# Stage 3 of a fused attention and gating kernel: leftover columns, product outputs and gate steps issued in another order

## The chip, the cores and the metric

The kernel runs on one core of a Trainium2 chip. The metric is the device time of one execution in microseconds; the kernel before took 685.45 us (median of 3 runs, 685.35 to 686.27). Every matmul is in 32-bit floats or in pairs of rounded high and low parts, so that a product of two such pairs is three matmuls.

## The reference

Three layers run one after the other on 4 batches of 576 rows. The change lies in the third.

```python
def reference(**kwargs):                      # cut
    attn_out = _attn_ref(q, k, v)             # rotary attention, 8 heads of 64
    x = _moe_ref(x=x, ...)                    # gated MLP with mixing over the rows
    return _moe2_ref(x=x, ...)

def _moe2_ref(x, w_gate, wq, wk, wv, wo):     # 4 experts, head width 64
    logits = x @ w_gate                       # the two best experts of each row, softmax over them: w
    for e in range(E):
        q, k, v = x @ wq[e], x @ wk[e], x @ wv[e]
        scores = scale * (q @ k.T), causal    # 576 x 576
        a = softmax(scores)
        ye = a @ v @ wo[e]
        out += (mask of e) * w * ye
```

## The kernel before

Stage 3 works through 8 units, n = 0 to 7: unit n is batch n // 2 and one pair of its four experts. A unit has 9 slots, x = 0 to 8, one for each block of 128 query rows of an expert (rows 512 to 575 of both experts share block 8). `slot3` writes out slot k = 9n + x. In it, in this order: `exps` of block x (ScalarE), the parked second halves of side products (`after`: evictions from PSUM, which also start the DMAs that fill q and k of the next unit), `scores` of block x + 1 and `turn` of block x - 1 (TensorE; the turn transposes the exponentials through a PSUM tile ps_t, of which there are two), `masked` of block x + 1 (VectorE: mask and maximum), `high` and `low` of block x - 1 (ScalarE copies the turned block to h1h or h0xh, VectorE writes the rounding error to h1l or h0xl). Then come the steps with the previous unit p, side products of other units (projections to q and k into the single two-bank tile ps_S, to values into ps_f and others, the output product into ps_f, ps_o or ps_S) and a few steps of the gates.

What the change touches:

- `gather` (VectorE) copies block 8's 64 leftover columns beside themselves, `turn_left` (TensorE) transposes them into a ps_t tile, `left_parts` makes the tile ht from them (ScalarE copy, VectorE subtraction). In the previous unit's block 8 this happens in slots 0 and 1.
- `av(True, 0)` and `av(True, 1)` are the second-half products with the values for the two experts of unit p, in slots 1 and 3; ps_o is a single PSUM tile. `av_out` empties it: ScalarE copies half of it to tmp, VectorE adds tmp to the other half, into xt. The last matmul of an `av` reads ht.
- `factor` makes the row factors rs (ScalarE, VectorE, four small GpSimd products with the gates wgt); `turn_factor` transposes them into ps_o's spare columns; `spread_factor` copies them to rr (ScalarE), stores rr in DRAM (d<-rr) and loads it back spread over the partitions (three DMAs r<-d).
- `finish(0)` and `finish(1)` (GpSimd) multiply xt by r and write the parts zh and zl, in slots 4 and 5 (unit 1: in 7 and 8). The output product `Output.blocks` reads them; in units 2, 4 and 6 its first two blocks, of the batch just ended, are side products of slots 6 and 7.
- `vproj` ends in seven steps for the gates: a subtraction (GpSimd), two comparisons (VectorE), two reductions and a subtraction into wgt (VectorE, GpSimd), an exponential of wgt (ScalarE), two more on VectorE, a sum and reciprocal, a product (GpSimd). Units 2, 4 and 6 run one step a slot.

ScalarE, VectorE, GpSimd and TensorE keep the order in which the program issues their instructions (the `Engine` wrapper pins it). DMAs issued on SP are not pinned in stage 3: a planner places each in SP's queue when it takes the DMA's inputs to be ready, the earlier in the program first. The queue itself runs in order, and a DMA that waits holds those behind it.

Unit 2 differs from units 3 to 7 in where its q and k projections stand: `QK_AT` spreads them over slots 0, 1, 3, 3, 4, 4, where the others have them in slots 0, 0, 2, 2, 3, 3. So in unit 2 half of a projection (6 matmuls) stands in slot 1, none in slot 2, and q is evicted (hi by ScalarE, lo by VectorE, then six DMAs q<-hi, qz<-hi, q<-lo) in slot 2, where the others do it in slot 1.

Of the kernel before, what the change touches and what calls it, by code (L numbers as in the profile page):

```python
# [15 lines left out]
B, H, S, D = 4, 8, 576, 64  # L16
# [27 lines left out]
def fused_kernel(ctx, tc, qk, v, w_in, w_out, w_sg, g_ln, b_sg, wqk, wvg, wo, rope, cst, out):  # L44
# [27 lines left out]
    def bank(t):  # L72
        shape = [P, 2, 512] if t.isupper() else [P, 512]
        return ps[t].tile(shape, F32, tag="b", name="ps_" + t)
# [195 lines left out]
    def parts_of(b):  # L270

        ts = []

        def load(c):
            t = xtile[0]()
            nc.sync.dma_start(t[:, 0:S], yd[b][c])
            nc.sync.dma_start(t[:, S:640], yd[b][c][:, 512:S])
            ts.append(t)

        for c in range(2):  # L280
            load(c)
            yield
        yp[b] = [ypools[b % 2].tile([P, 4, 640], F32R, tag="y" + x, name="y" + x) for x in "hl"]
        for c in range(4):
            split(yp[b][0][:, c], yp[b][1][:, c], ts[c])
            if c < 2:
                load(c + 2)
            yield
# [57 lines left out]
    with ExitStack() as st:  # L346
# [279 lines left out]
        works = {0: Work(), 1: Work()}  # L626
# [28 lines left out]
        for k in range(9 * B * NP + 7):  # L655
            n, x = divmod(k, 9)
# [27 lines left out]
    def qkproj(n, x):  # L684

        b, pp = divmod(n, 2)
        yh, yl = yp[b]
        hi = one.tile([P, S], F32R, tag="hi", name=f"hi{x}")
        lo = (ld if x else one).tile([P, S], F32R, tag=f"lo{x}", name=f"lo{x}")
        sl = slice((2 * x + pp) * P, (2 * x + pp) * P + P)  # L690
        t = bank("S")
        for x_ in mm3(halves(t), [(wq[0][:, c, sl], wq[1][:, c, sl], yh[:, c], yl[:, c]) for c in range(4)]):
            if n:
                yield
        if n == 0:
            yield
        pv = t[:, :, 0:HS]
        if x == 0:
            ACT.activation(hv(hi), pv, AF.Copy, scale=0.125)
            DVE.scalar_tensor_tensor(hv(lo), pv, 0.125, f(hv(hi)), op0=ALU.mult, op1=ALU.subtract)  # L700
            prs3[pp].fill_q(hi, lo)
        else:
            ACT.copy(hv(hi), pv)
            DVE.tensor_tensor(hv(lo), pv, f(hv(hi)), op=ALU.subtract)
            prs3[pp].fill_k(ld, hi, lo)
        yield
# [251 lines left out]
    with ExitStack() as st:  # L958
# [10 lines left out]
        def load_sel():  # L969

            for i in range(2):
                t0 = xtile[0]()
                t = t0[:, 0:3 * P]
                nc.sync.dma_start(t, cst[:, P + 928 + 3 * P * i:P + 928 + 3 * P * i + 3 * P])
                sel.extend(t[:, P * x:P * x + P] for x in range(3))
                blank.append(t0[:, 512:640])
                POOL.memset(blank[i], 0.0)
# [276 lines left out]
                d.tensor_tensor(zl[:, self.pp, c], self.xt[:, c], f(zh[:, self.pp, c]), op=ALU.subtract)  # L1254

        works, qk, vp, op, gate, ys = {}, {}, {}, {}, [], []
        after = []

        def step(g):

            if g is not None:
                next(g)
                after.append(g)

        def slot3(k):

            n, x = divmod(k, 9)
            (nk, xk), (nn, xn) = divmod(k - 1, 9), divmod(k + 1, 9)
            if xn == 0 and nn < 2 * B:
                works[nn] = Causal(nn)  # L1270
            w, p, wk_, wn = [works.get(i) for i in (n, n - 1, nk, nn)]
            b, pp = divmod(n, 2)
            last = n == 2 * B - 1
            if last and x == 0:
                load_sel()
            late = 4 if n == 1 else 1

            def values():

                for at, g, second, j in ((1, p, True, 0), (2 if last else 3, p, True, 1),  # L1280
                                         (6 if last else 4, w, last, 0), (7 if last else 5, w, last, 1)):
                    if g and x == at:
                        g.av(second, j, "f" if last and at == 2 else "o")
                        if at == late and p:
                            p.turn_factor(g.o[:, 320:448])
                            p.spread_factor()
                        elif last and at == 7:
                            w.turn_factor(w.o[:, 320:448])
                            w.copy_factor()
                        g.av_out(second, j)  # L1290


            if w:
                w.exps(w.order[x])
            for g in after:
                next(g, None)
            after.clear()
            if last and x == 7:
                w.part_factor(True)
            if wn:  # L1300
                wn.scores(wn.order[xn])
            if wk_:
                wk_.turn(wk_.order[xk])

            if wn:
                wn.masked(wn.order[xn])
            if wk_:
                wk_.high(wk_.order[xk])
                wk_.low(wk_.order[xk])
            if p and x == 0 and p.n < 2 * B - 1:  # L1310
                p.gather()
            if last and x == 5:
                w.gather()
            if p and x == late - 1:
                for i in range(3):
                    p.factor(i)
            if p and x == 1:
                p.turn_left()
                p.left_parts()
            if x != 1 and not (last and x > 5):  # L1320
                values()
            fx = (3, 4) if last else FINISH_AT[n != 1]
            if p and x in fx:
                p.finish(fx.index(x))

            if w:
                if x == 8 and n + 2 < 2 * B:
                    qk[n + 2, 0] = qkproj(n + 2, 0)
                at = FIRST_QK_AT if n == 0 else QK_AT if n == 2 else (0, 0, 2, 2, 3, 3)
                if x == at[2] and n + 1 < 2 * B:  # L1330
                    qk[n + 1, 1] = qkproj(n + 1, 1)
                for i, y in enumerate((8, 8) + at):
                    g = qk.get((n + 2, 0) if i < 2 else (n + 1, i // 4))
                    if x == y and g is not None:
                        next(g)
                        if i in (3, 7):
                            after.append(g)
                if pp == 0 and x in (6, 7) and b > 0:
                    if x == 6:
                        op[b - 1] = Output(b - 1).blocks()  # L1340
                    step(op[b - 1])
                if x in ((0, 4, 6) if last else (1, 4, 5) if pp == 0 and b > 1 else ()):
                    step(op[b - 2 if pp == 0 else b - 1])
                if pp == 1 and b + 1 < B and x in (1, 4, 5, 6, 7):
                    if x == 1:
                        vp[b + 1] = vproj(b + 1)
                    step(vp[b + 1])
                if n == 0 and x in VALUES_AT:
                    step(vp[0])
                elif last:  # L1350
                    if x == 7:
                        op[b] = Output(b)
                        t = bank("S")
                        op[b].t = {2: t[:, 0], 3: t[:, 1]}
                        for tb in (2, 3):
                            op[b].product(tb, op[b].t[tb], 0)
                    if x == 8:
                        for tb, t in ((4, "f"), (0, "s")):
                            op[b].t[tb] = bank(t)
                            op[b].product(tb, op[b].t[tb], 0)  # L1360
                        w.spread_here(True, "s")
                        w.finish(1, False)
                        w.av(False, 0)
                        w.av_out(False, 0)
                elif pp == 0 and b > 0:
                    next(vp[b], None)
                for _ in range(GATES_AT.get(k, 0)):
                    next(vp[0], None)
            if last and x == 6:
                w.turn_left()  # L1370
                w.left_parts()
            if x == 1 or last and x > 5:
                values()

            if (n + 1) // 2 + 1 < B:
                if k == 0 or pp and x == 0:
                    ys.append(parts_of((n + 1) // 2 + 1))
                if x in INPUT_AT[min(n, 2 - pp)]:
                    next(ys[-1], None)
# [11 lines left out]
        for k in range(18 * B):  # L1391
            slot3(k)
        w, g = works[2 * B - 1], op[B - 1]
# [103 lines left out]
```

## Time and profile before

| what | value |
| --- | --- |
| median of 3 runs | 685.45 us |
| the profiled execution's own time | 685.67 us |
| its span in the trace | 683.9 us |
| TensorE busy | 669.8 us (98%) |
| VectorE, ScalarE, GpSimd busy | 453.8, 428.7, 343.5 us |
| stage 3, from its first score product | from about 503 us to the end |

TensorE's share is read with care: matmuls are pipelined and their ends are modelled, so the waits in the chain of waits and the starts in the timeline say more than the busy share. In the lines of the trace an operation is named by what it writes and reads: `e<-ps_s,mask` is `masked`, `e<-e,nmax` is `exps`, `ps_t<-ident,e` is a turn, `ps_S<-kh,q` is the scores of block 8, `ps_S<-w,zh` and `ps_f<-w,zh` are output products, `xt<-ps_o,tmp` ends `av_out`. All have the line of a helper, L58. SPq is SP's queue of DMA issues; PEld loads TensorE's weights.

### The profile page before, as it was taken

Reading aid. Unit: us, or ns where it says so; the run is one execution under the profiler, and the core shown is the slowest. Engines: PE = TensorE matmul, PEld = TensorE weight load, DVE = VectorE, ACT = ScalarE, POOL = GpSimd, SP = SyncE. Lnnn points to the kernel's source line nnn. Section 1 sums busy time; section 2 is a strip of 40 time slices with the busy share of each in tenths; the row PEclk is TensorE's granted clock in tenths of the full one; section 3 lists DMA queues with packets and bytes.
Section 4 is the critical chain, followed back from the end, with each engine's and each line's share of the span. In section 5 each row is a group of like instructions: output and inputs, shape, how many; then the busy total and the mean of one; then the engine's idle time right before and its main releaser. Section 6 shows DMA issues by size and latency. Waiting matters only on the chain.

```text
span 683.9 us, 13699 instructions
## 1 busy us (share of the span) xinstructions
PE 669.8 (98%) x4781; PEld 588.2 (86%) x4781; DVE 453.8 (66%) x1026; ACT 428.7 (63%) x1050; POOL 343.5 (50%) x333
## 2 busy tenths in 40 slices
PE   6999999999999999999999999999999999999997
PEld 6777777777777777799999999999999989999985
DVE  5777777777777867478964764664247666556673
ACT  6577776767777777564472473472156676666674
POOL 1886777778888861562446227206223443342320
PEclk9799999999999999999999999999999999999999
DMA  8588887888788762652465233055455364443522
GB/s 301 162 252 255 233 257 203 245 242 255 222 238 256 224 179 84 184 160 79 117 186 176 87 118 119 17 139 158 126 163 142 92 171 103 124 134 77 139 83 77
DMA packets 65538, 112.47 MB, mean 164 GB/s; under 512 B 20527, under 2 KB 25726, under 8 KB 65470
## 3 DMA queue, kind: packets, MB, share of 16 engines
q1 hardware_dynamic: 62734, 105.92, 53.6%
q10 hardware_dynamic: 2736, 5.68, 2.8%
q8 instruction: 38, 0.62, 0.4%
q14 instruction: 30, 0.25, 0.1%
HBM read 58.32 MB, written 18.98 MB: 113 GB/s over the span
## 4 chain that ended last, share of the span: by engine, by line
PE 89%; DVE 5%; ACT 4%; issue 1%; DMA 1%; SPq 0%; ACTq 0%; DVEq 0%
PE ps_S L58 48%; PE ps_o L58 17%; PE ps_t L58 14%; PE ps_f L58 5%; PE ps_s L58 3%; PE ps_l L58 2%; DVE nmax L58 1%; ACT qz L58 1%; ACT e L58 1%; DVE ga L58 1%; DMA x<-yd 1%; ACT ga L58 0%; ACT vh L58 0%; DVE g L58 0%; DVE q L58 0%
## 5 line engine op out<-in xcount | busy, mean ns | idle before, releaser
L58 ACT ACTIVATE e<-ps_S,nmax 128x576 f32<-128x576 f32 x144 | 108.0, 750 | 70.7 <-DVE nmax L58 70.1
L58 DVE TENSOR_REDUCE nmax<-ps_S 128x1 f32<-128x576 f32 x144 | 108.7, 755 | 58.0 <-PE ps_S L58 55.7
L58 PE MATMUL ps_t<-ident,e 128*128 128x128 f32 x776 | 122.0, 275 | 1.2 <-ACT e L58 0.7
L58 PEld LDWEIGHTS ps_t<-ident,e 128*128 128x128 f32 x776 | 95.8, 141 | 5.4 <-ACT e L58 1.3
L58 POOL TENSOR_TENSOR t<-t,rp 128x576 f32<-128x576 f32 x61 | 85.4, 1422 | 15.0 <-ACT rp L58 9.2
L58 PE MATMUL ps_S<-kh,q 128*128 128x288 f32 x352 | 88.0, 343 | 4.7 <-ACT kh L58 2.9
L58 PEld LDWEIGHTS ps_S<-kh,q 128*128 128x128 f32 x352 | 54.5, 193 | 33.3 <-issue 10.2
L58 PE MATMUL ps_o<-g,v 128*64 128x320 f32 (+1 forms) x512 | 76.2, 418 | 0.0
L58 POOL TENSOR_TENSOR lo<-t,hi 128x576 fp32r<-128x576 f32 x30 | 43.2, 1440 | 49.0 <-DVE hi L58 49.0
L58 PE MATMUL ps_S<-lo,qz 128*128 128x288 f32 x304 | 66.5, 300 | 1.4 <-DVE lo L58 1.4
L58 PEld LDWEIGHTS ps_o<-g,v 128*64 128x64 f32 x512 | 31.3, 136 | 24.2 <-issue 9.5
L58 PE MATMUL ps_S<-yh,w 128*128 128x288 f32 x256 | 51.8, 304 | 0.0
L58 PEld LDWEIGHTS ps_S<-lo,qz 128*128 128x128 f32 x304 | 49.8, 193 | 1.7 <-DVE lo L58 1.7
L58 ACT ACTIVATE e<-e,nmax 128x128 f32<-128x128 f32 (+4 forms) x72 | 42.2, 586 | 13.6 <-DVE nmax L58 13.4
L58 POOL TENSOR_TENSOR yl<-x,yh 128x640 fp32r<-128x640 f32 x16 | 26.0, 1630 | 47.7 <-ACT yh L58 47.7
L58 ACT COPY g<-ps_t 128x512 f32<-128x512 f32 x80 | 46.7, 584 | 3.0 <-PE ps_t L58 2.4
L58 DVE COPY g<-ps_t 128x512 f32<-128x512 f32 x64 | 43.6, 681 | 1.4 <-PE ps_t L58 1.3
L58 POOL TENSOR_TENSOR t<-t 128x576 f32<-128x576 f32 x29 | 41.4, 1427 | 2.3
L58 PEld LDWEIGHTS ps_S<-yh,w 128*128 128x128 f32 x256 | 38.7, 189 | 0.0
L58 ACT ACTIVATE ga<-ga 128x512 f32<-128x512 f32 (+1 forms) x34 | 22.3, 656 | 25.5 <-DVE ga L58 25.5
L58 PE MATMUL ps_S<-wsh,vh 128*128 128x288 f32 x160 | 34.6, 297 | 0.8 <-DVE u L58 0.5
L58 POOL TENSOR_TENSOR gxl<-u,gxh 128x576 fp32r<-128x576 f32 x16 | 22.8, 1434 | 24.0 <-ACT gxh L58 24.0
(290 smaller groups left out, 1751.3 us busy)
## 6 DMA issues: line engine op xcount, KB each, us to landing
t<-in_qk_dram SPq DMA_DIRECT2D x32, 576.0 KB
kh<-hi SPq DMA_DIRECT2D x92, 144.0 KB
q<-hi SPq DMA_DIRECT2D x38, 144.0 KB
qz<-hi SPq DMA_DIRECT2D x38, 144.0 KB
q<-lo SPq DMA_DIRECT2D x38, 144.0 KB
v<-in_v_dram SPq DMA_DIRECT2D x16, 320.0 KB
sa<-xr SPq DMA_DIRECT2D x16, 288.0 KB
xd<-sa SPq DMA_DIRECT2D x16, 288.0 KB
```

The lines of the kernel that those rows point to most:

```text
L58: ins = op(*a, **k)
```

## The change

- `gather` is issued ahead of `high` and `low` of slot 0 instead of behind them.
- `turn_left` and `left_parts` are issued at the end of slot 1, behind its side products and just ahead of `av(True, 0)`, instead of ahead of the side products.
- In slot 1 of units 1 to 6, `av_out` of the product and (units 2 to 6) `spread_factor` are put into a list `rest`, which slot 2 runs behind its exponentials, its evictions and `masked`, and ahead of `high` and `low`.
- `finish(1)` of unit 0's results is issued in slot 0 of unit 2, behind `factor`, instead of in slot 8 of unit 1.
- The gates' steps in units 2, 4 and 6 begin in slot 2 instead of slot 0, one a slot as before, and so end in slot 8 instead of slot 6.

```diff
-        after = []
+        after, rest = [], []
...
                         if at == late and p:
                             p.turn_factor(g.o[:, 320:448])
-                            p.spread_factor()
+                            (rest.append if x == 1 and not last else lambda do: do())(p.spread_factor)
...
-                        g.av_out(second, j)
+                        if x == 1 and not last:
+                            rest.append(lambda g=g, second=second, j=j: g.av_out(second, j))
+                        else:
+                            g.av_out(second, j)
...
             if wn:
                 wn.masked(wn.order[xn])
+            if p and x == 0 and p.n < 2 * B - 1:
+                p.gather()
+            for do in rest:
+                do()
+            rest.clear()
             if wk_:
                 wk_.high(wk_.order[xk])
                 wk_.low(wk_.order[xk])
-            if p and x == 0 and p.n < 2 * B - 1:
-                p.gather()
...
             if p and x == late - 1:
                 for i in range(3):
                     p.factor(i)
-            if p and x == 1:
-                p.turn_left()
-                p.left_parts()
+                if n == 2:
+                    works[0].finish(1)
...
-            if p and x in fx:
+            if p and x in fx and (n, x) != (1, 8):
                 p.finish(fx.index(x))
...
-                elif pp == 0 and b > 0:
+                elif pp == 0 and b > 0 and x > 1:
                     next(vp[b], None)
...
+            if p and x == 1:
+                p.turn_left()
+                p.left_parts()
             if x == 1 or last and x > 5:
                 values()
```

## Rows read from the trace of the kernel before

**Rows 1.** The page's first part: busy time of the engines.
```profile
PE 669.8 (98%) x4781; PEld 588.2 (86%) x4781; DVE 453.8 (66%) x1026; ACT 428.7 (63%) x1050; POOL 343.5 (50%) x333
```
**Rows 2.** Chain of waits, slot 1 of unit 2: start us, us, what.
```profile
544.97 0.30 PE ps_t L58
545.27 0.80 PE ps_S L58 x6
```
**Rows 3.** Timeline, TensorE, unit 2: start, us, engine, instruction, [idle before, releaser].
```profile
544.23 0.27 PE L58 MATMUL ps_t<-ident,e 128*128 128x128 f32 x1
...
548.73 0.20 PEld L58 LDWEIGHTS ps_t<-ident,e 128*128 128x128 f32 x2 [1.03 <-ACT e L58]
...
548.92 0.78 PE L58 MATMUL ps_o<-h1h,vst 128*128 128x320 f32 x4
```
**Rows 4.** Timeline, ScalarE, slots 1 and 2 of unit 2.
```profile
545.30 0.27 ACT L58 CAST ht<-ps_t 128x128 fp32r<-128x128 f32 x1 [0.50 <-PE ps_t L58]
...
547.63 0.42 ACT L58 COPY tmp<-ps_o 64x320 f32<-64x320 f32 x1
...
548.08 0.51 ACT L58 ACTIVATE e<-e,nmax 128x256 f32<-128x256 f32 x1
...
548.70 0.65 ACT L58 ACTIVATE hi<-ps_S 128x576 fp32r<-128x576 f32 x1
```
**Rows 5.** Timeline, VectorE, slot 2 of unit 2.
```profile
548.08 0.48 DVE L58 TENSOR_TENSOR xt<-ps_o,tmp 64x320 f32<-64x320 f32 x1 [0.72 <-ACT tmp L58]
...
549.38 0.76 DVE L58 SCALAR_TENSOR_TENSOR lo<-ps_S,hi 128x576 fp32r<-128x576 f32 x1 [0.82 <-ACT hi L58]
...
550.06 0.41 DVE L58 CUSTOM_DVE_ANT_0 e<-ps_s,mask 128x256 f32<-128x256 f32 x1
```
**Rows 6.** Timeline of SP's queue: unit 2 (first two), unit 3 (the rest).
```profile
547.63 0.29 SPq L197 DMA_DIRECT2D d<-rr  x1
548.90 0.45 SPq L201 DMA_DIRECT2D r<-d  x1
...
566.03 0.47 SPq L169 DMA_DIRECT2D q<-hi  x1
...
569.80 0.46 SPq L197 DMA_DIRECT2D d<-rr  x1
571.86 0.46 SPq L201 DMA_DIRECT2D r<-d  x1
```
**Rows 7.** Timeline, GpSimd, `finish(0)` in unit 2 (two rows) and unit 3 (one).
```profile
553.28 0.73 POOL L58 TENSOR_TENSOR xt<-xt,r 128x256 f32<-128x256 f32 x1 [0.49 <-DMA r<-d]
...
554.56 0.74 POOL L58 TENSOR_TENSOR zl<-xt,zh 128x256 fp32r<-128x256 f32 x1
...
576.03 0.74 POOL L58 TENSOR_TENSOR xt<-xt,r 128x256 f32<-128x256 f32 x1 [8.65 <-DMA r<-d]
```
**Rows 8.** Timeline, TensorE, output product in slot 6 of unit 2, second half.
```profile
557.37 0.63 PE L58 MATMUL ps_f<-w,zh 128*128 128x512 f32 x2
557.84 0.40 PE L58 MATMUL ps_f<-w,zl 128*128 128x512 f32 x1
```
**Rows 9.** Timeline, unit 6: a gate step, ScalarE's slot 6, `finish(0)`'s end, next ps_S product.
```profile
639.96 0.22 POOL L58 TENSOR_TENSOR wgt<-lg,m 128x20 f32<-128x20 f32 x1 [3.81 <-DVE m L58]
...
646.47 0.71 ACT L58 ACTIVATE e<-e,nmax 128x512 f32<-128x512 f32 x1
...
647.09 0.74 POOL L58 TENSOR_TENSOR zl<-xt,zh 128x256 fp32r<-128x256 f32 x1
...
647.47 0.58 ACT L58 COPY ob<-ps_S 64x512 f32<-64x512 f32 x1 [0.20 <-PE ps_S L58]
...
649.48 0.71 PE L58 MATMUL ps_S<-kh,q 128*128 128x288 f32 x4
```
**Rows 10.** Timeline, unit 4: the same end of `finish(0)` and the same ps_S product.
```profile
600.14 0.74 POOL L58 TENSOR_TENSOR zl<-xt,zh 128x256 fp32r<-128x256 f32 x1
...
603.84 0.71 PE L58 MATMUL ps_S<-kh,q 128*128 128x288 f32 x4
```

## The prediction

> **What bounds the kernel now.** The page comes first: TensorE is busy for 98% of the span, the next engine for 66% [rows 1]. So only time in which TensorE stands still can be won or lost. The chain of waits says where that is: in stage 3, from its first scores to the last unit's end phase, its pieces are TensorE's, except around one place, the first slots of unit 2. There the timeline shows two waits. The first: the turn of block 0 starts at 544.23 and the next TensorE instruction, `turn_left`, only at 544.97, because it needs the gathered columns, and the gather stands on VectorE behind `low` [rows 2, 3]. The second: a turn in slot 3 starts at 548.73 after its weight load stood 1.03 us for the exponentials of slot 2 [rows 3]; these started at 548.08, in ScalarE's queue right behind the copy tmp that empties ps_o (547.63 to 548.05) [rows 4]. The change aims at both. What it can win is bounded by them; what it can lose lies in what is pushed back instead, wherever TensorE waits for that.
>
> **The change part by part.** The sums go against the profiled execution, 685.67 us; the median of the runs is 0.22 lower, and the differences are added to the median.
>
> *Gather ahead of `low`, `turn_left` behind the side products.* No instruction is added. Between the two starts at 544.23 and 544.97 lie 0.74 us; the turn itself is modelled at 0.27, so between 0.47 and 0.74 is lost, and I take 0.6. The six side matmuls (0.80, [rows 2]) now fill this, and `turn_left` comes after them, at about 545.2. The gather's place on VectorE costs nothing, since `low` waits there for ScalarE. Behind `turn_left` the copy to ht now has only the eight matmuls of `av` as cover: the transpose 0.30 [rows 2], the copy 0.27 [rows 4] and a subtraction of the same tile (the copy's length is my estimate for it) make about 0.85, and four `av` matmuls alone take 0.78 [rows 3], eight some 1.3. That leaves 0.4 us of slack, and I cost it at nothing; if VectorE or ScalarE came late, a few tenths in each of six units would be lost.
>
> *Output behind the exponentials.* The exponentials of slot 2 no longer stand behind rr and tmp, so the 1.03 us in front of the turn goes. But `av(True, 1)` in slot 3 needs the single tile ps_o, and what empties it now stands behind the exponentials, and in unit 2 behind the eviction of q as well, since that unit evicts in slot 2. I add up the new chain. Side products from about 544.42 (behind the turn, 0.6 early by the step above) for 0.80: 545.22. `turn_left` 0.30 and ht 0.27: 545.79. Exponentials, 0.62 from start to the next start (548.08 to 548.70): 546.41. hi 0.65: 547.06, during which the product ends and tmp then needs 0.42, so VectorE is later: lo, 0.68 from start to next start (549.38 to 550.06): 547.74. `masked` 0.41: 548.15. The sum into xt 0.48: 548.63 [rows 2, 4, 5]. `av(True, 1)` started at 548.92 before [rows 3]. So 0.3 of the 1.6 us of both waits is won: a wait for ps_o takes the place of the wait for exponentials. Bounds: 0 if VectorE is a little later, 1.6 (0.6 and 1.03) if ps_o were free in time.
>
> In the other units the exponentials (0.62) and one eviction or store (at most 0.65 [rows 4]) now precede, up to 1.3 us, but there 12 projection matmuls, twice the 0.80 [rows 2], stand in slot 2 and cover it. Priced at nothing; if the cover fell short, it would be a tenth or two a unit.
>
> *What `spread_factor` is pushed behind.* This is where I expect the loss. In unit 2, d<-rr is issued now at 547.63, with SP idle, and the q fills follow the r loads. In the changed program the eviction precedes `spread_factor`, so the six fills come first: hi is ready at 547.06, before rr on the same engine. Unit 3 already has this order: from its first fill at 566.03 to d<-rr at 569.80 are 3.77 us, from there to the first r load 2.06, from there to `finish(0)` on GpSimd 4.17 (576.03) [rows 6, 7]. Applied to unit 2: first fill 547.06, d<-rr 550.83, r load 552.89, `finish(0)` 557.06 instead of 553.28. `finish(0)` needs 1.28 until zh is written (zl starts at 554.56) and 2.02 until zl is (555.30) [rows 7], so zh is there at 558.34, zl at 559.08. The output product of slot 6 reads them for its second half, zh at 557.37 and zl at 557.84 before, 0.3 earlier now: 557.07 and 557.54 [rows 8]. Today's slack of some 2.5 us is used up, and TensorE stands until 559.08 instead of 557.54: 1.54 us lost. Bounds: nothing, if the planner puts d<-rr ahead of the fills; 2.3 if loads behind fills take as much longer again as d<-rr does (the 0.79 below).
>
> The way from d<-rr to the r load took 1.27 us in unit 2, with a quiet queue, and 2.06 in unit 3, behind fills [rows 6]. With 1.27 the loss would be 0.75, with 2.06 it is 1.54. The Trainium skill (DMA: Bandwidth & Descriptors, section on latency and other measured facts) says that a DMA's fixed cost is mostly the round trip to memory and grows with the load on HBM; both rows agree, and by that rule the later place, behind fills, pays the larger figure.
>
> *Gate steps two slots later.* The subtraction into wgt moves to slot 4, on GpSimd behind `finish(0)`, and the exponential of wgt on ScalarE to slot 5: ScalarE, in order, waits in slot 5 for `finish(0)`, and its exponentials, stores and `high` wait behind. In unit 6 zl ends at 647.83; the subtraction 0.22 and an exponential of the same 20 columns (0.2, estimated from it) bring 648.25 instead of 646.47 for the next exponentials; the store from ps_S started 1.00 behind these, so 649.25, and ends 0.58 later, 649.83; the scores of block 8 need ps_S at 649.48 [rows 9]. Loss 0.35, between 0.15 (the store's own wait of 0.20 falls away) and 0.75 (the r loads are also pushed behind an output store, by some 0.4, about one issue [rows 6]). In unit 4 the same steps end at 600.88 + 0.42 + 1.00 + 0.58 = 602.88, ahead of 603.84 [rows 10]: nothing. In unit 2 ScalarE waits too, but TensorE is by then held by zl itself.
>
> *`finish(1)` of unit 0 behind `factor`.* Three GpSimd operations swap places with the row factors, which `turn_factor`, now 0.6 earlier, needs sooner; its own result is read two units later. Nothing.
>
> Sum: -0.3 + 1.54 + 0.35 = +1.59 us, from 685.45 to 687.0.
>
> **The rivals.**
> 1. *The factor is stored in time.* The planner puts d<-rr behind the four fills from hi and ahead of the two from lo, or ahead of all. With four fills (four sixths of 3.77, 2.5) d<-rr goes at 549.57, zl is there at 557.82, 0.28 late; ahead of all, nothing is late. Then -0.3 to 0, with unit 6's 0.35: 685.2 to 685.8. For it: SP's order isn't the program's. Against it: in unit 3 all six went first.
> 2. *Both waits simply go.* ps_o is emptied in time and the factor too: 1.6 less, 683.8 to 684.3. It needs `masked` and lo out of the way of xt, which the order in slot 2 does not give; it decides as soon as the sum into xt ends before the two short turns behind `av(True, 0)` do.
> 3. *The cover in slots 1 to 3 of the other units is too short* (ht or ps_o late by 0.1 to 0.3 in five or six units): 1 us more beside the forecast, 688.
>
> **How the numbers follow.** Forecast 0.55, its own range 686.3 to 687.8; rival 1 0.33; rival 2 0.07; rival 3 0.05. The measurement can tell about 0.2%, 1.37 us, from no change. The forecast's +1.59 lies just beyond this, and its range lies on both sides, some six parts in ten beyond: slower 0.33 + 0.05, rounded up to 0.40 for waits in the same place that I under-price; faster 0.08; same 0.52. A range from 685.0 to 687.8 leaves out rival 2, most of rival 3 and the edges, under 2 in 10.
>
> **What would show it.** Right: around 544 in unit 2 no gap before `turn_left`; the turn of slot 3 without a wait for exponentials, but the following `av` waiting for xt; on SP six fills ahead of d<-rr in unit 2; a gap on TensorE of 1 to 2 us at the output product of unit 2's slot 6, released by zh or zl; in unit 6 ScalarE waiting for wgt and the scores of block 8 for the store ob. Wrong: d<-rr ahead of the fills, or `finish(0)` of unit 2 starting within 10 us of the gather; then the time stays at 685.5. A gap at an `av`'s last matmul in units 3 to 6 would be rival 3.

## The result and the profile after

The changed kernel takes 689.01 us in the median of five executions (686.64 to 689.80; a sixth, at 733.91 us and with a granted clock of 0.85, was disturbed and is left out, and with it the median is 689.20), the kernel before 685.35 in six executions beside it. The ratio is 1.0052, with a 95% interval from 1.0039 to 1.0065: by the ratio some 3.6 us slower, where 687.0 was forecast. The profiled execution took 689.01 us with a span of 687.2, against 685.67 and 683.9.

The page's first part shows 2.4 us more busy time on TensorE for the same 4781 instructions [rows 1]:

```profile
PE 672.2 (98%) x4781; PEld 589.7 (86%) x4781; DVE 455.3 (66%) x1026; ACT 428.6 (62%) x1050; POOL 343.7 (50%) x333
```

That is the first thing to notice: nothing was added to TensorE, so the same matmuls must have taken longer.

TensorE's waits in stage 3, by what ended them (total us, times, longest):

```profile
PE ps_f L58 <- POOL zh L58: 1.5, 1, 1.5
PE ps_o L58 <- DVE xt L58: 1.0, 1, 1.0
```

Both are new. The two waits of the kernel before at which the change aimed, for the exponentials of slot 2 and before `turn_left`, are gone:

```profile
PE ps_t L58 <- ACT e L58: 0.7, 1, 0.7
PE ps_t L58 <- DVE rs L58: 0.5, 1, 0.5
```

SP's queue in unit 2 of the kernel after (start us, us) has the six q fills ahead of the factor's store d, and its load r behind that [rows 6]:

```profile
546.45 0.48 SPq L169 DMA_DIRECT2D q<-hi  x1
...
548.97 1.17 SPq L169 DMA_DIRECT2D q<-lo  x2
550.56 0.29 SPq L197 DMA_DIRECT2D d<-rr  x1
...
552.79 0.47 SPq L201 DMA_DIRECT2D r<-d  x1
```

GpSimd, the same unit: `finish(0)` starts at 556.94, the forecast having 557.06 [rows 7]:

```profile
556.94 0.72 POOL L58 TENSOR_TENSOR xt<-xt,r 128x256 f32<-128x256 f32 x1 [6.39 <-DMA r<-d]
```

TensorE: the first row answers to the product of slot 3 [rows 3], the others to the output product of slot 6 and what follows it [rows 8]:

```profile
548.27 0.77 PE L58 MATMUL ps_o<-h1h,vst 128*128 128x320 f32 x4 [1.03 <-DVE xt L58]
...
558.18 0.73 PE L58 MATMUL ps_f<-w,zh 128*128 128x512 f32 x2 [1.50 <-POOL zh L58]
559.00 0.50 PE L58 MATMUL ps_f<-w,zl 128*128 128x512 f32 x1
559.34 1.01 PE L58 MATMUL ps_S<-kh,q 128*128 128x288 f32 x4
```

The four score matmuls of the last row take 0.71 at the same form elsewhere [rows 9]; here they take 1.01. The windows of one microsecond say why. Their columns are length, the busy time of TensorE, its weight loads, VectorE, ScalarE and GpSimd, then the granted TensorE clock, DMA share and GB/s:

```profile
558.00:559.00 1.00, 0.73 (x3) 0.30 (x3) 0.00 (x0) 0.00 (x0) 0.92 (x3) 1.00 1.00 217
559.00:560.00 1.00, 1.00 (x5) 0.96 (x6) 0.00 (x0) 0.84 (x4) 1.00 (x2) 0.75 0.07 16
560.00:561.00 1.00, 1.00 (x6) 0.98 (x5) 0.52 (x2) 1.00 (x4) 1.00 (x2) 0.50 0.00 0
561.00:562.00 1.00, 1.00 (x6) 0.90 (x5) 0.90 (x4) 0.92 (x4) 0.91 (x2) 0.50 0.45 81
562.00:563.00 1.00, 1.00 (x4) 0.81 (x3) 1.00 (x4) 0.92 (x3) 0.88 (x1) 0.54 0.85 287
563.00:564.00 1.00, 1.00 (x8) 0.87 (x8) 0.25 (x3) 0.62 (x3) 0.23 (x1) 1.00 0.64 227
```

The granted clock falls to 0.50, the lower of its two levels (1.2 GHz), at about 559.5, 1.3 us behind the end of the wait, and stays there for 3.4 us, while TensorE is fully busy (0.75 and 0.54 stand for windows that hold both levels). The page's line of 40 slices can't show this: a slice is 17 us, and its digit there is 9. In the kernel before these windows all have 1.00. What the fall costs is read from the chain of waits (start us, us, what), after and then before:

```profile
559.50 1.33 PE ps_S L58 x6
560.83 0.85 PE ps_t L58 x4
561.68 2.02 PE ps_o L58 x6
```

```profile
558.24 0.80 PE ps_S L58 x6
559.03 0.44 PE ps_t L58 x4
559.47 1.40 PE ps_o L58 x6
```

The same sixteen instructions take 4.20 us instead of 2.64, 1.56 us more.

In unit 6 the gate exponential waits on ScalarE, and the exponentials, the store and the scores that need ps_S come behind it [rows 9]; first ScalarE, then TensorE:

```profile
651.28 0.22 ACT L58 ACTIVATE wgt<-wgt 128x20 f32<-128x20 f32 x1 [1.82 <-POOL wgt L58]
...
652.11 0.56 ACT L58 COPY ob<-ps_S 64x512 f32<-64x512 f32 x1
```

```profile
652.72 0.80 PE L58 MATMUL ps_S<-kh,q 128*128 128x288 f32 x4
```

**The account.** Stage 3's first scores start 0.36 earlier in this execution (502.75 against 503.11), ahead of anything that the diff touches, so the shifts are counted from there. The product of slot 3 moved from 548.92 to 548.27: 0.29 won. The scores behind the output product start at 559.50 instead of 558.24 in the chain: from the point reached, 1.26 + 0.36 + 0.29 = 1.91 lost to the wait. The slow clock: 1.56. Unit 4: 0.15 (these scores start at 606.72 instead of 603.84 and take 0.80 instead of 0.71, 2.97 in all, of which 1.26 + 1.56 = 2.82 was there already). Unit 6: 0.33. Together 3.66, less the 0.36 of the start: 3.30, which is the difference of the spans.

### The profile page after: what moved, and what is told of

It reads as the page before. It is cut to its first block, busy times and chain, and to the rows that moved or that the text cites. A ratio compares the mean times of both kernels' runs of the same rounds, so it can differ in the third digit from the quotient of the medians.

```text
span 687.2 us, 13690 instructions
## 1 busy us (share of the span) xinstructions
PE 672.2 (98%) x4781; PEld 589.7 (86%) x4781; DVE 455.3 (66%) x1026; ACT 428.6 (62%) x1050; POOL 343.7 (50%) x333
## 4 chain that ended last, share of the span: by engine, by line
PE 86%; DVE 4%; ACT 4%; DMA 2%; POOL 1%; issue 1%; SPq 1%; ACTq 0%; POOLq 0%; DVEq 0%
PE ps_S L58 47%; PE ps_o L58 17%; PE ps_t L58 13%; PE ps_f L58 5%; PE ps_s L58 3%; PE ps_l L58 2%; ACT qz L58 1%; DVE nmax L58 1%; ACT e L58 1%; DMA sa<-xr 0%; DMA sr<-rd 0%; DMA r<-d 0%; POOL sa L58 0%; POOL x L58 0%; DVE ga L58 0%
## 5 line engine op out<-in xcount | busy, mean ns | idle before, releaser
L58 DVE CUSTOM_DVE_ANT_0 e<-ps_s,mask 128x128 f32<-128x128 f32 (+3 forms) x64 | 31.0, 485 | 12.9 <-PE ps_s L58 10.9
L58 POOL TENSOR_TENSOR xt<-xt,r 128x256 f32<-128x256 f32 (+1 forms) x14 | 11.3, 807 | 48.9 <-DMA r<-d 48.9
```

The costliest lines, as they stand in the source:

```text
L58: ins = op(*a, **k)
```

## The experiments

My theory after this: the change loses by the factor's place behind the q fills, once by the wait in slot 6 of unit 2 and once more by the clock that falls behind it. Rivals: the gate steps or the deferred output lose the time, and the wait in slot 6 is only where it shows; or the clock falls anyway and costs nothing of its own.

**The queue's order alone** (`sp_order`). The kernel after, with only the q fills of slot 2 in unit 2 held back:

```
             for do in rest:
                 do()
             rest.clear()
+            for o, i in late_fills:      # cut: fill_q collects them in slot 2 of unit 2
+                tc.keep_in_program_order(nc.sync.dma_start(f(o), f(i)))
```

> The changed kernel with one thing different: in unit 2 the six q fills are queued on SP behind d<-rr and the r loads instead of ahead of them; all compute engines keep the changed kernel's order. Theory (the queue place of d<-rr is the cause: TensorE waits 1.9 us for zh and zl, and then runs some 3 us at half the granted clock, 1.5 us more): finish(0) of unit 2 starts at 551 to 553 instead of 556.9, no gap before the output product of slot 6, granted clock 1.00 throughout, 3.3 to 3.5 us back, 685.3 to 685.9 us; units 4 and 6 keep their 0.15 and 0.33. Rival (the gate steps moved behind finish(0) hold ScalarE, whatever the queue does): ScalarE's order is untouched, so at most 1 us comes back, 688 to 689.

Measured 686.05 (684.59 to 687.50), ratio 1.0014 [1.0005, 1.0023], span 684.4: 0.15 above the theory's range, far below the rival's. SP's queue and GpSimd's `finish(0)`:

```profile
546.89 0.29 SPq L202 DMA_DIRECT2D d<-rr  x1
548.14 0.45 SPq L206 DMA_DIRECT2D r<-d  x1
...
549.98 0.53 SPq L1323 DMA_DIRECT2D q<-hi  x1
```

```profile
552.37 0.74 POOL L58 TENSOR_TENSOR xt<-xt,r 128x256 f32<-128x256 f32 x1 [1.58 <-DMA r<-d]
```

`finish(0)` is 4.6 us earlier than after, TensorE's wait for zh is gone, the clock stays at 1.00, and 2.8 of the 3.3 us between the spans of after and before are back, where the theory had 3.3 to 3.5. The store and the load of the factor stand 1.25 us apart here, 2.23 behind the fills. The Trainium skill (DMA: Bandwidth & Descriptors, section on latency and other measured facts) has a DMA's fixed cost grow with the load on HBM. These two rows, like the prediction's two, agree in direction only: the fills copy from tile to tile in SBUF, and no run here measures the load on HBM. A part of the longer way is queueing: by the trace's packets the store's nine run 0.8 us behind its issue in unit 2 of the kernel before, and in unit 3, among the last packets of the fills, 1.2 to 1.4 behind it.

What is left over before, 1.0 us by the ratio and 0.5 by the spans, is in unit 6, where the scores wait for the store behind the gate exponential:

```profile
649.96 0.79 PE L58 MATMUL ps_S<-kh,q 128*128 128x288 f32 x4 [0.87 <-ACT ob L58]
```

Counted by TensorE's starts against before, unit 6 loses 1.1 us here and 0.33 in the kernel after, and unit 4 loses nothing, so the theory's 0.15 and 0.33 did not hold as they stood. The ps_o wait of slot 3 (1.03, as after) is no part of it: the product behind it starts 0.30 earlier than before, counted from the stage's start (548.51 for 548.92, 503.00 for 503.11).

**Work in the gap** (`filler`). The kernel after with six more matmuls into the waiting output product, which then start it anew, so that the wait is filled and its end stays where it was:

```
+                    for _ in range(2 if (self.b, tb) == (0, 0) else 0):
+                        self.product(tb, t, 0, True)      # cut: with True the sum ends there
                     for c in range(2):
                         self.product(tb, t, c)
```

> The changed kernel with work added: in unit 2's slot 6 the first half of the first output product, three matmuls of 512 columns, is run twice more ahead of itself, 6 extra matmuls of about 0.23 us, 1.4 us, in the stretch in which TensorE waits for zh. Theory (the fall of the granted clock behind the wait is a cost of its own): TensorE is idle for at most some 0.3 us at a time, the granted clock stays 1.00 from 557 to 564, and the kernel with more work is 1.3 to 1.6 us faster than the changed one, about 687.6. Rival (the products behind the wait are long because ScalarE and VectorE are late with what they read): the stretch from 559 to 563 is as long as in the changed kernel and the time stays at 689 or rises.

Measured 687.44 (687.10 to 688.49), ratio 1.0037 [1.0024, 1.0049]: more matmuls than the kernel after, and 1.6 us less, by the medians (689.01) as by the spans (685.6 for 687.2). zl is as late as in the kernel after (559.07 against 559.00), the wait for zh is down to 0.24, and the scores behind take 0.69 again, not 1.01:

```profile
558.25 0.73 PE L58 MATMUL ps_f<-w,zh 128*128 128x512 f32 x2 [0.24 <-POOL zh L58]
559.07 0.50 PE L58 MATMUL ps_f<-w,zl 128*128 128x512 f32 x1
559.40 0.69 PE L58 MATMUL ps_S<-kh,q 128*128 128x288 f32 x4
```

All windows from 556 to 564 have a clock of 1.00. So the fall is a cost of its own, beside the wait, and it stays away when TensorE has work there.

**The left columns alone** (`left_only`). The kernel before with gather ahead of `high` and `low`, and `turn_left` and `left_parts` behind the side products (the diff's lines for these, nothing else):

> The kernel before with only the leftover columns' part: gather ahead of low, turn_left and left_parts behind the side products. Theory: the wait before turn_left in unit 2 goes and nothing takes its place, since exponentials, rr and tmp all move forward with the product: 0.5 to 0.6 us less than before, 684.8; no wait at the last matmul of av in any unit. Rival (ht comes late for av's last matmul): 0.1 to 0.3 us lost in each of six units, 685.5 to 687.

Measured 686.84 (686.27 to 687.80), ratio 1.0026 [1.0016, 1.0037]: it loses where a gain was expected, by as much as the rival said, though not evenly over the units. VectorE in slot 1 of unit 2, and the last matmul of the product, which reads ht:

```profile
546.90 0.24 DVE L58 SCALAR_TENSOR_TENSOR eq<-cmp,lower 128x80 f32<-128x80 f32 x1 [1.88 <-POOL cmp L58]
547.18 0.24 DVE L58 SCALAR_TENSOR_TENSOR cmp<-cmp,eq 128x80 f32<-128x80 f32 x1
547.46 0.29 DVE L58 TENSOR_TENSOR ht<-ps_t,ht 64x128 fp32r<-64x128 f32 x1
```

```profile
547.80 0.30 PE L58 MATMUL ps_o<-ht,vst 128*128 128x64 f32 x1 [1.59 <-DVE ht L58]
```

The subtraction into ht now stands behind a gate step's two comparisons, and these wait for GpSimd, where cmp comes after `finish(1)` of unit 0 and the row factors. ht is 1.6 us late in unit 2; in units 4 and 6, the others with gate steps, the same matmul comes 0.2 late. The later gate steps of the change take these comparisons out of slot 1; `left_gates` below tries that.

**The gate steps back** (`gates_early`). The kernel after with one condition undone:

```
-                elif pp == 0 and b > 0 and x > 1:
+                elif pp == 0 and b > 0:
```

> The changed kernel with the gate steps back in slots 0 to 6. Theory: unit 2 still loses its wait for zh and the clock behind it (nothing there but GpSimd and SP decides), units 4 and 6 win back about 0.5 us: 688.3 to 688.9. Rival (gate steps are the cause): 685.4 to 686.

Measured 688.90 (688.58 to 690.43), ratio 1.0059 [1.0047, 1.0072], as slow as the kernel after and at the top of the theory's range, but not by the theory's wait. The same row as in the last experiment, and the clock behind it:

```profile
548.90 0.30 PE L58 MATMUL ps_o<-ht,vst 128*128 128x64 f32 x1 [2.76 <-DVE ht L58]
```

```profile
551.00:552.00 1.00, 1.00 (x5) 1.00 (x5) 0.83 (x5) 0.72 (x3) 0.74 (x2) 0.50 0.96 200
```

`finish(1)` stands behind the factor here, so cmp is later still (547.65 on GpSimd) and ht 2.76 us late. The clock is at 0.50 for 6.8 us here, from 549.95 to 556.78, twice as long as in the kernel after. This profile is of the slowest execution, at 690.43; the other four, from 688.58 to 689.02, have none. The wait for zh in slot 6 does not appear in this trace at all: TensorE comes so late to slot 6 that the late factor is covered. An equal time does not mean an equal cause.

**The deferred output alone** (`out_only`). The kernel before with `av_out` of slot 1 put off behind the next exponentials, evictions and masked step:

```
-                        g.av_out(second, j)
+                        if x == 1 and not last:
+                            rest.append(lambda g=g, second=second, j=j: g.av_out(second, j))
+                        else:
+                            g.av_out(second, j)
```

> The kernel before with one part of the change: in slot 1 the evacuation of the product's output (av_out) waits until the next exponentials, the evictions and the masked step are issued; the factor still leaves at once, gather, turn_left, the gate steps and finish(1) stand as before. Theory (the deferral pays only in unit 2, where the trace after shows the second product start 0.29 us sooner, and the loss of the change comes from the factor's place in the queue): 684.7 to 685.3. Rival (the output buffer ps_o comes free later in every unit, and TensorE waits for it): 686.0 or more, with waits of ps_o for VectorE's xt in several units.

Measured 687.93 (686.65 to 688.90), ratio 1.0036 [1.0023, 1.0050]: the theory's value is missed and the rival's size is met. Most of it is in unit 2. Counted by TensorE's starts against before, the product of slot 3 comes another 0.30, 0.09, 0.32 and 0.14 late in units 3 to 6, which it does not in the kernel after. ScalarE, then TensorE in unit 2:

```profile
545.90 0.26 ACT L58 COPY rr<-ps_o 9x128 f32<-9x128 f32 x1 [1.79 <-PE ps_o L58]
546.06 0.51 ACT L58 ACTIVATE e<-e,nmax 128x256 f32<-128x256 f32 x1
```

```profile
548.98 1.30 PE L58 MATMUL ps_o<-h1h,vst 128*128 128x320 f32 x4 [1.83 <-DVE xt L58]
```

The factor's copy rr stays ahead of the exponentials and waits for the product's end, so the exponentials start 0.16 behind rr, where in the kernel after they start 1.09 ahead of it (545.28, and rr at 546.37). The eviction and the output come behind them, and the second product waits 1.83 us for its tile. Its four matmuls take 1.30 instead of 0.78 [rows 3]: half clock again, from 549.0 to 552.4.

**The factor at once, the rest as after** (`spread_now`). The kernel after with `p.spread_factor()` called in slot 1 instead of being appended to `rest`:

> The kernel after with one edit of the change undone in every unit: the factor's copy and its four DMAs are issued in slot 1 at once, and only the output's evacuation waits for the next exponentials. Theory (all of the loss but a few tenths is the factor's place behind the six q fills of unit 2): no zh wait in slot 6 of unit 2, clock 1.00 there, 685.2 to 686.1, as with the queue's order alone. Rival (the output's later evacuation costs by itself, as it did on the kernel before where its wait of 1.8 us brought half clock): 687.0 to 688.0, with a ps_o wait of 1.5 us or more in slot 3 of unit 2.

Measured 688.23 (686.45 to 689.74), ratio 1.0042 [1.0028, 1.0056]: the rival, 0.23 above its range. The factor is in time and nothing waits for zh, but the wait of `out_only` is back, 1.89 us:

```profile
546.42 0.26 ACT L58 COPY rr<-ps_o 9x128 f32<-9x128 f32 x1 [0.98 <-PE ps_o L58]
546.58 0.50 ACT L58 ACTIVATE e<-e,nmax 128x256 f32<-128x256 f32 x1
```

```profile
549.55 0.77 PE L58 MATMUL ps_o<-h1h,vst 128*128 128x320 f32 x4 [1.89 <-DVE xt L58]
```

In the kernel after the exponentials start at 545.28, in `spread_now` at 546.58, with the stage's start 0.06 later. So deferring the factor's copy is what lets the exponentials go ahead; without it, deferring the output only makes the output late, in units 3 to 6 too (0.80 there, as in `out_only`).

**The deferred factor alone** (`factor_only`). The kernel before with only `spread_factor` put off:

> The kernel before with one edit of the change done alone: the factor's copy and its four DMAs wait until the next exponentials, evictions and masked step are issued (d and r then stand behind the six q fills in unit 2); the output is evacuated at once, gather, turn_left, gate steps and finish(1) stand as before. Theory (the late factor by itself makes TensorE wait in slot 6 of unit 2, and the clock falls behind that wait): PE waits 1.3 to 2.2 us for zh and zl there, at least one stretch with a granted clock of 0.6 or less between 558 and 564 us, 687.9 to 689.2. Rival (the loss needs the other edits too, finish(1) and the later gate steps on GpSimd): 685.2 to 686.2 with a wait below 0.5 us.

Measured 691.12 (690.75 to 691.40), ratio 1.0088 [1.0075, 1.0102]: the direction and place of the theory, but 2 us beyond its range. SP, GpSimd and TensorE in unit 2:

```profile
553.36 0.29 SPq L197 DMA_DIRECT2D d<-rr  x1
```

```profile
560.03 0.72 POOL L58 TENSOR_TENSOR xt<-xt,r 128x256 f32<-128x256 f32 x1 [7.34 <-DMA r<-d]
```

```profile
561.26 1.09 PE L58 MATMUL ps_f<-w,zh 128*128 128x512 f32 x2 [3.39 <-POOL zh L58]
```

The fills themselves start only at 549.25 here, not at 546.45, because the exponentials and the eviction still stand behind the output copy; so d is 2.8 us later than after (0.5 of it because stage 3 starts later), and the wait 3.39 instead of 1.50.

**The left columns with the gate steps** (`left_gates`). `left_only` with the diff's gate condition and with `finish(1)` of unit 0 behind the factor; factor and output at once:

> The kernel before with the left columns' part (gather early, turn_left and left_parts behind the side products) and with the gate steps two slots later and finish(1) of unit 0 behind the factor, but with the factor and the output taken at once, as before. Theory (the left columns alone lost 1.4 us because two gate comparisons on VectorE, which wait for GpSimd behind finish(1), stood ahead of the left parts' subtraction; the later gate steps take them away): no ht wait over 0.3 us in slot 1 of unit 2, 685.2 to 686.0, the remainder over before being the gate exponential's waits in units 4 and 6 (0.15 and 0.33). Rival (moving the left columns costs by itself, VectorE or TensorE short in slot 1): 686.6 to 687.2, as left_only.

Measured 684.68 (683.88 to 685.25), ratio 0.9993 [0.9984, 1.0001], span 683.5: better than the theory's 685.2 to 686.0. The ht wait is gone; the longest wait of TensorE in stage 3 is the old one for the exponentials, 0.7 us, and unit 6 loses 0.2.

**Output first** (`out_first`, and `both` with the gate steps shifted in unit 2 only). The kernel after with the deferred work run right behind the exponentials, output ahead of factor:

```
             if w:
                 w.exps(w.order[x])
+            for do in rest[::-1]:      # cut: taken from behind `masked`
+                do()
+            rest.clear()
             for g in after:
                 next(g, None)
```

> The kernel after with the deferred work (output, then factor) run right behind the exponentials, the gate steps two slots later in units 2, 4 and 6 as in the change. Theory (units 4 and 6 lose 0.15 and 0.33 us to the gate exponential behind finish(0), nothing else): 0.3 to 0.6 us slower than the same kernel with the shift in unit 2 only, 684.2 to 685.1. Rival (those small waits are covered): the same time as that kernel.

> The kernel after with the deferred work (output, then factor) run right behind the exponentials, ahead of the pending evictions, so that the factor's d goes ahead of the q fills in unit 2; and with the gate steps two slots later in unit 2 only. Theory: the zh wait of unit 2 (1.91), its half clock (1.56), the ps_o wait (1.03) and the ScalarE waits of units 4 and 6 (0.15 and 0.33) are all gone, and none takes their place: 683.7 to 684.6, faster than both kernels. Rival 1 (units 4 and 6 then wait for ht, since the gate comparisons stand ahead of the left parts again): 684.6 to 685.4. Rival 2 (the exponentials' slot is now short on ScalarE, the output copies delay the evictions and with them the scores): 685.4 or more.

Measured 684.90 (684.09 to 685.78), ratio 0.9997 [0.9988, 1.0006], span 683.1; and 685.01 (684.05 to 685.44), ratio 0.9994 [0.9985, 1.0003], span 683.2. The two don't differ, as the rival of `out_first` had it, and `both` misses its theory (683.7 to 684.6) and lies in its rival 1. In both, d goes ahead of the fills, and of the ps_o wait of 1.03 there is left one of 0.4 (released by rr), TensorE's longest in stage 3. Again equal times have unlike causes: counted by TensorE's starts against before, `out_first` loses 0.2 in unit 6, at the scores behind the gate exponential, and `both` loses 0.2 in unit 4 and 0.2 in unit 6 at the matmul that reads ht, as its rival 1 had it.

The two spans are 0.8 and 0.7 below that of before, of which 0.36 and 0.44 are an earlier start of stage 3, and neither these two nor `left_gates` has an interval wholly below 1, so none is shown to beat the kernel before; all three beat the change.

**The same kernels again** (`out_again`, `now_again`). The times of `out_only` and `spread_now` each fell into two groups, so each was profiled once more, unchanged:

> The kernel with only the output's evacuation deferred, once more, for one time together with its profile. Its five times before fell into two groups, 686.65 and 686.68 against 687.93 to 688.90, and the one profile (687.93) shows half clock from 549 to 553 us behind a wait of 1.83 us. Theory (the wait is in every execution, the fall of the clock only in some, and the fall is what parts the two groups): the wait is again 1.8 us; with half clock behind it the time is 687.9 to 688.9, with the clock at 1.00 it is 686.4 to 686.9. Rival (the clock falls every time and the groups part elsewhere): half clock with a time below 687, or full clock with a time above 687.8.

> The kernel after with the factor taken at once and only the output deferred, once more, for one time together with its profile. Its six times before: 686.45, 686.73 and 687.97 to 689.74; the profile of the 688.49 one shows half clock from 551 to 554 us behind a wait of 1.89 us. Theory (the clock's fall parts the groups): the same wait of 1.9 us; with half clock 687.9 to 689.8, with the clock at 1.00 686.4 to 686.8. Rival (it falls every time): half clock with a time below 687, or full clock with a time above 687.8.

`out_again` took 688.95 us (expected 687.9 to 688.9 at half clock), with the 1.83 us wait and half clock behind it. `now_again` took 687.16 (expected 686.4 to 686.8 at full clock, so 0.4 above), and it is the telling one: the wait is the same 1.89 us, and the clock does not fall. One window behind the wait, of `now_again` and then of `spread_now`:

```profile
551.00:552.00 1.00, 1.00 (x9) 1.00 (x9) 0.50 (x2) 0.98 (x3) 0.14 (x1) 1.00 0.72 210
```

```profile
551.00:552.00 1.00, 1.00 (x5) 1.00 (x5) 0.41 (x1) 0.86 (x3) 0.07 (x1) 0.50 0.75 230
```

And a product of slot 7, in the same order, which follows without another wait:

```profile
559.72 0.72 PE L58 MATMUL ps_o<-w,zh 128*128 128x512 f32 x2
```

```profile
561.22 0.71 PE L58 MATMUL ps_o<-w,zh 128*128 128x512 f32 x2
```

The wait ended at 549.62 in the first and 549.55 in the second, the product starts 1.50 later in the second: the fall costs 1.57 us here, beside 1.56 in the kernel after, and it is not in every execution. This also fits the lone 686.64 of the kernel after among times from 688.38 to 689.80, whose granted clock over the whole execution is on record as 0.995, the others' as 0.990 to 0.994. But that execution has no profile, so for it the cause is only argued.

## Why the prediction was wrong

Most steps came out as written. SP has six fills ahead of d; `finish(0)` of unit 2 is at 556.94 for 557.06; the wait for exponentials is gone and one for xt stands in its place, 0.29 won for 0.3; unit 6 loses 0.33 for 0.35. That `finish(0)` came so close is in part luck: the first fill went 0.61 earlier than forecast (546.45 for 547.06), but from it to d are 4.11 us and not 3.77, and from d to the load 2.23 and not 2.06. Rival 1 (the factor stored in time) is what `sp_order` builds, and its time of 685.2 to 685.8 ends 0.25 below what that measured. Rivals 2 and 3 did not come: TensorE does wait for xt, and units 3 and 5 of the kernel after lose nothing. The two waits that the prediction put at 1.6 us together are 1.2 by TensorE's own idle time (0.7 and 0.5 in the lines of the kernel before above; the 1.03 is that of the weight load), which lowers a bound and not the sum. And that both of its rows agree with the Trainium skill's rule on the load on HBM was read too strongly, as `sp_order` shows; the 2.06 itself came from a row, and 2.23 was measured.

The step that failed is the price of the wait in *What `spread_factor` is pushed behind*: "TensorE stands until 559.08 instead of 557.54: 1.54 us lost", with 2.3 as its upper bound. The mechanism and the place were right, the size was not. The wait itself cost 1.91: TensorE came 0.36 earlier than forecast, since stage 3 began earlier, while GpSimd was only 0.12 earlier, which makes 0.24 of the 0.37; another 0.10 is the product with zl, 0.50 for 0.40 [rows 8]. But the larger miss is a term that the sum did not have. Behind the wait the clock fell to its lower level for 3.4 us, which cost 1.56 us in the profiled execution. So the row of the sum is 3.47 and not 1.54, and `filler` and the pair of `now_again` and `spread_now` show that the two parts are separate. With the measured terms the sum is -0.29 + 1.91 + 1.56 + 0.15 + 0.33 = 3.66, or 689.1 instead of 687.0, for 689.0 in the median. In stage 3 the trace of before shows nothing of the kind: TensorE's longest wait there, 0.7 us, left the clock at 1.00. But its first 25 us do, in rows that the prediction did not use. TensorE waits 2.94 us, just behind that the clock goes from 1.00 to 0.50, and there, with two shorter waits on the way, it stays until 24.4:

```profile
13.91 0.60 PE L58 MATMUL ps_S<-kh,q 128*128 128x288 f32 x2 [2.94 <-ACT kh L58]
```

```profile
13.00:14.00 1.00, 0.09 (x1) 0.12 (x2) 0.94 (x3) 0.87 (x2) 0.00 (x0) 1.00 0.57 99
15.00:16.00 1.00, 0.12 (x1) 0.12 (x1) 0.79 (x2) 0.00 (x0) 0.00 (x0) 0.50 1.01 415
```

So what the prediction lacked is an upper bound that lets what follows a new wait run at half clock for a while, and a reason to expect one was in the trace. That a wait of 1.5 us is enough, it could not tell from there.

Unit 4 was costed at nothing and lost 0.15: the sum kept `finish(0)` where it was, but there too it came later, zl starting at 604.32 for 600.14 [rows 10], 1.4 more than the 2.82 lost until then. The slack of ht, 0.4 us, was right only by grace of the gate steps' shift, which I had read as a pure cost: "if VectorE or ScalarE came late" is what happened without it, 1.59 us in one unit (`left_only`). And the two deferrals were costed one by one, though each changes what the other costs: alone they lose 2.8 and 6.0 us in the median, together and with the rest of the change 3.7.

## What to carry to other kernels

A new wait of TensorE is priced at its own length and, as an upper bound, at a stretch of half clock behind it: here 1.5 to 1.9 us of waiting brought another 1.6 us in four profiled executions of six, and the 2.76 us of `gates_early` a stretch of half clock twice as long. When work is pushed back on one engine, follow every in-order queue that it feeds: here a copy of 0.25 us moved behind an eviction put its store behind six fills, and its reader 3.7 us later. And when single edits of a change are tried alone, an edit that looks like a cost may be what keeps another in time.

## What the runs showed that I had not expected

The clock's answer to a wait is not settled by the wait alone. Behind 1.50 us (the kernel after), 1.83 (`out_only` and `out_again`), 1.89 (`spread_now`), 2.76 (`gates_early`) and 3.39 (`factor_only`) it fell to 0.50; behind 1.59 (`left_only`, followed by another wait of 0.71) and the very same 1.89 of `now_again` it stayed at 1.00. Where it fell, it did so between 0 and 1.3 us behind the end of the wait, and for 3.4 us, in `gates_early` 6.8. What parts the cases no run here decides. It makes one profile of such a kernel a draw: `spread_now` and `now_again` are one program with spans of 686.7 and 685.4.
